# A gated attention and GLU kernel, forward and backward: 34 far attention tiles turned by DMA, filler work spread over the query tiles, K and V in rings of two

## The chip, the cores and the metric

The kernel runs on one core of a Trainium2 chip. The metric is the device time of one execution in microseconds (us); lower is better. The core's engines are TensorE (PE in the profile; its weight loads are PEld), VectorE (DVE), ScalarE (ACT), GpSimd (POOL) and SyncE (SP). SP computes nothing: it issues most of the DMAs, one after the other in the order in which they were written.

## The reference

The program computes a layer's output and the gradients of seven of its inputs. Batch 1, S = 2048 tokens, D = 512, H = 32 heads of 16, attention window W = 256, F = 1376; all in bfloat16.

```python
def A(x, wqkv, wo):                       # sliding-window attention
    q, k, v = (x @ wqkv) split into 32 heads of 16
    scores = q k^T * 16 ** -0.5, kept where 0 <= i - j < 256, else -1e9
    return (softmax(scores) v) @ wo
def B(x, W_gate, W_up, W_down):           # gated MLP
    gate, up = x @ W_gate, x @ W_up
    return (gate * (gate > 0) * up) @ W_down
g = sigmoid((x * gate_w).sum(-1))
out = g * A(x) + (1 - g) * B(x)
# returned: out, and the gradients for grad_out of x, wqkv, wo, W_gate, W_up, W_down, gate_w
```

## The kernel before, in words

There are three stages, one after the other. Their PE work is laid end to end by hand-written lists (`manual_schedule`): every engine executes its instructions in the order in which Python emits them.

**Stage 1 (0 to about 250 us), the MLP.** 44 steps of 128 features by 512 tokens: gate, up, the gradient of h, and the weight gradients. Its last steps also make the first projections for the attention.

**Stage 2 (about 250 to 715 us), the attention forward and backward.** The heads are worked through in four groups c = 0 to 3 of 8 heads, in each 16 query tiles j of 128 tokens. A query tile meets up to three key tiles kb: its own (role d, kb = j), the one before (role m, j - 1) and the far one (role f, j - 2; masked from the other side). Each pair is done in two halves of four heads. One half of one pair is a *unit*; there are 360, six for a full query tile.

A unit runs through these steps, one new unit per round n of the loop:

- round n: `front` (L681) multiplies K by Q into PSUM (ST, PE), ACT takes the exponential into the tile Pu, POOL masks it for the roles d and f;
- round n + 1: `front_dp` (L704) multiplies V by the output's gradient (dPT, PE);
- round n + 2: `gradp` (L712), DVE multiplies Pu by dPT into Pd;
- round n + 4: `rowsum` (L717), row sums, outputs and query gradients (BA), eight small matmuls;
- Pu and Pd have to be turned (keys on the rows, queries on the columns exchanged) for the key and value gradients. `flip` (L735) does it. The two halves of a d pair and of an m pair lie side by side and are turned by one DMA transpose from SP (L743, 128x2048, in round n + 3 of the second half). Far units, and four m units at the end of the last group, are turned by PE: eight 128x128 transposes into PSUM (L753) and one eviction by ACT or DVE (L754, L755), in round n + 4.
- `cd_piece` (L532) multiplies the turned tiles by the small tensor rq into CD, the sums for the key and value gradients of one key tile. A key tile needs its three query tiles; the six pieces are put in a queue `cdq` with the round from which they may run, and one or two are taken per round.

Between the units the loop places *filler work* for PE. `project_parts` (L123) makes the six parts of the next projection: Q, dO, a DMA transpose of rows, K, V, and the transposes for KV1. They belong to a *block* of four query tiles (512 tokens of one head group; 16 blocks in all), and one block ahead is projected. `grad_parts` (L627) makes the gradient of wqkv and wo for the head group before: four sums of four pieces, each piece four matmuls (L641), and a store after each sum.

What is placed when is decided by a `credit`: each round adds 1.5 us, less what the unit itself costs (0.63, and 0.44 where PE turns a tile), and each filler takes its own cost from it. A projection part is taken when the credit is over 0.4 and one round was left free, or when its due round comes; a gradient piece when at most two projection parts are left (L960). `plan` (L620) says after which block's projection which weights of stage 3 are turned or loaded into the slots x0..x3, d0..d3, p0..p3, which the inputs of projections no longer needed leave free; `late` holds them, and they are issued in some rounds only (L966). The rest, `W_rest`, follows after the attention.

The projected K0, K1, V0, V1 and KV1 lie in rings: every third block's in the pool pjA (one buffer), the others' in the pool `pj` (two buffers), so three blocks are alive at a time (L126, L518). The far units have rings Pu and Pd of two buffers each, and their turned tiles P2f a ring of four.

**Stage 3 (about 715 us to the end)** multiplies h by Wdown and o by its gradient, then, per token tile, computes the output and the gradient of x.

Of the kernel before, what the change touches and what calls it, by code (L numbers as in the profile page):

```python
# [11 lines left out]
BF = mybir.dt.bfloat16  # L12
# [10 lines left out]
def kernel(  # L23
# [20 lines left out]
    nc = tc.nc  # L44
    P = 128
# [9 lines left out]
    NT = S // P  # L55
# [56 lines left out]
    if True:  # L112
# [10 lines left out]
        def project_parts(c, tg):  # L123
            t4 = {}
            proj[(c, tg)] = t4
            pj = lambda: pjA if (c * NTG + tg) % 3 == 0 else pjs["b"]  # L126

# [386 lines left out]
    if True:  # L514
        st = p3.enter_context(tc.tile_pool(name="attst", bufs=2))
        gwp = p3.enter_context(tc.tile_pool(name="gwp", bufs=2))
        p3b = ExitStack()
        pjs["b"] = p3b.enter_context(tc.tile_pool(name="pj", bufs=2))  # L518
        wk = p3b.enter_context(tc.tile_pool(name="attw", bufs=2))
# [63 lines left out]
        def clear(name):  # L583
            nc.gpsimd.memset(W6[(name, FC - 1)][0:FC * P - F, :], 0.0)
# [32 lines left out]
        def load_gw():  # L617
# [4 lines left out]
                12: turns("Wg", B_W_gate, 0, 4, "x0") + turns("Wg", B_W_gate, 4, 8, "d0"),  # L622
                15: loads("Wd", B_W_down, 0, "x3") + loads("Wd", B_W_down, 4, "d3") + loads("Wd", B_W_down, 8, "p3")}
        W_rest = (turns("Wg", B_W_gate, 8, 12, "x1") + [lambda: clear("Wg")] + turns("Wu", B_W_up, 0, 4, "d1") + turns("Wu", B_W_up, 4, 8, "x2")
                  + turns("Wu", B_W_up, 8, 12, "d2") + [lambda: clear("Wu")])

# [35 lines left out]
        for c in range(DC):  # L662
            for j in range(NT):
                kbs = [k for k in (j - 1, j, j - 2) if k >= 0]
                for half in range(2):
                    order = kbs if half or len(kbs) < 3 else [kbs[0], kbs[2], kbs[1]]
                    for ki, kb in enumerate(order):
                        u = Unit()
                        u.c, u.j, u.kb, u.half = c, j, kb, half
                        u.first = ki == 0 and half == 0  # L670
                        u.last = ki == len(kbs) - 1 and half == 1
                        u.role = ("d", "m", "f")[j - kb]
                        u.pair = u.role == "d" or (u.role == "m" and (c < DC - 1 or j < NT - 2))
                        u.own = u.role == "f"
                        u.dma = u.pair
                        units.append(u)
# [4 lines left out]
        def front(u):  # L681
# [6 lines left out]
            if not u.own:  # L688
                if u.half == 0:
                    tag = f"PP{u.role}"  # L690
                    pairs[(u.c, u.j, u.kb)] = wk.tile([P, 2, 2, HH, P], BF, tag=tag, bufs=3, name=tag)
                u.PP = pairs[(u.c, u.j, u.kb)][:, u.half, :, :, :]
                u.Pu, u.Pd = u.PP[:, 0, :, :], u.PP[:, 1, :, :]
            else:
                u.Pu = wk.tile([P, HH, P], BF, tag="Pu", bufs=2, name="Pu")
            nc.scalar.activation(u.Pu[:], ST[:], ACT.Exp)  # L696
# [15 lines left out]
        def gradp(u):  # L712
            if u.own:
                u.Pd = wk.tile([P, HH, P], BF, tag="Pd", bufs=2, name="Pd")
            nc.vector.tensor_tensor(out=u.Pd[:], in0=u.Pu[:], in1=u.dPT[:], op=ALU.mult)  # L715
# [19 lines left out]
        def flip(u):  # L735
            key = (u.c, u.j, u.kb, "p2")
            if u.role != "f" and key not in P2 and not (u.pair and u.half == 0):
                P2[key] = wk.tile([P, 2, 2, HH, P], BF, tag=f"P2{u.role}", bufs=3, name=f"p2{u.role}")
            if u.dma:
                if u.pair and u.half == 0:  # L740
                    return
                hs = slice(0, 2) if u.pair else slice(u.half, u.half + 1)
                nc.sync.dma_start_transpose(out=P2[key][:, hs, :, :, :].rearrange("p b a h q -> p (b a h) q"),  # L743
                                            in_=pairs[(u.c, u.j, u.kb)][:, hs, :, :, :].rearrange("p b a h q -> p (b a h q)"))
                for b in range(2)[hs]:
                    P2[(u.c, u.j, u.kb, b)] = P2[key][:, b, :, :, :]
                return
# [3 lines left out]
            for a, src in enumerate((u.Pu, u.Pd)):  # L751
                for hh in range(HH):
                    nc.tensor.transpose(pt[:, a, hh, :], src[:, hh, :], ident[:])  # L753
            p2 = P2[key][:, u.half, :, :, :] if u.role == "m" else wk.tile([P, 2, HH, P], BF, tag="P2f", bufs=4, name="p2")[:]  # L754
            evac(p2, pt[:], eng)  # L755
# [83 lines left out]
        with tc.manual_schedule():  # L839
# [36 lines left out]
            while n <= NU + LAG or ev or cdq or bgq:  # L876
                now = ev.pop(n, [])
                u = units[n] if n < NU else None
                if u is not None:
# [3 lines left out]
                    if u.first and u.j % TPG == 0:  # L883
                        if gi + 1 < len(groups):
                            prq = project_parts(*groups[gi + 1]) if gi else second
                            due = n + sum(2 * min(3, j + 1) for j in range(u.j, u.j + TPG)) - 3
                            if gi + 2 == len(groups):
                                due -= 10
                    if u.first and u.j == TPG and ends:
                        copies.append(ends.pop(0))  # L890
                    if u.first and u.j == 1 and u.c > 0:
                        ready = grad_parts(u.c - 1)
                    if u.first and u.j == TPG - 1 and u.c > 0:
                        bgq += ready
                    front(u)
# [51 lines left out]
                elif held and credit > 0.3:  # L947
                    held = background()
                    credit -= 0.65
                elif prq and not held and ((credit > 0.4 and n > fed + 1) or due - n <= len(prq)):  # L950
                    fed = n
# [6 lines left out]
                    if not prq:  # L958
                        late += plan.get(gi + 1, [])
                elif bgq and len(prq) <= 2 and credit > 0.3:  # L960
                    held = background()
                    credit -= 0.65
# [178 lines left out]
```

## Time and profile before

Three runs took 907.59, 908.57 and 911.35 us, the median is 908.57.

| What | Value |
|---|---|
| Profiled execution, its own time | 907.26 us |
| Its span, first to last instruction | 905.5 us |
| Granted TensorE clock | 1.00 throughout |
| PE busy | 889.5 us, 98% |
| DVE, ACT, POOL busy | 511.1, 445.5, 492.8 us |
| First and last score matmul (ST) of the attention | 249.6 and 697.5 us |
| Head groups 0 to 3, from first ST to the next group's first ST | 101.9, 115.5, 115.9, 114.6 us |
| DMA transposes of d pairs and of m pairs from SP | 64 and 58 |
| Their median time from issue to landing | 5.5 and 5.3 us |
| Transposes by PE of far units (L753) | 896, 112 units of 8 |

A row of the profile that names a line and an engine is a group of equal instructions: what it writes and reads, how many, the busy time, the mean duration in ns, and the idle time of the engine before them with what ended it. SPq is the DMA queue of SP; the duration of its rows is the time for which an issue holds the queue, not the time to the landing. The DMA share of a stretch adds up the times of all packets over 16 DMA engines and can be above 1, since packets overlap.

### The profile page before, as it was taken

How to read it: one execution, taken by the hardware profiler on the slowest of the kernel's cores; microseconds unless marked ns; L12 is line 12 of the kernel's file. 1: busy time of each engine (PE TensorE's matmuls, PEld its weight loads, DVE VectorE, ACT ScalarE, POOL GpSimd, SP SyncE). 2: the span in 40 equal slices, each digit the busy share in tenths (PEclk: the TensorE clock that was granted, in tenths of full speed). 3: DMA queues.
4: the chain of work that ended last, by engine and by line, in shares of the span. 5: the costliest groups of instructions: out<-in, count | busy, mean ns of one | idle time of the engine just before them, and what ended most of it. 6: DMA issues, size and time to landing. Idle time of an engine off the chain costs nothing.

```text
span 905.5 us, 25962 instructions
## 1 busy us (share of the span) xinstructions
PE 889.5 (98%) x10607; PEld 560.2 (62%) x10607; DVE 511.1 (56%) x946; ACT 445.5 (49%) x787; POOL 492.8 (54%) x937
## 2 busy tenths in 40 slices
PE   9999999999989999999999999999999999999998
PEld 5565655655657777677776677766677544444445
DVE  4433334434368887678886788877786101333343
ACT  6422232222278778667776677766787112111111
POOL 4544545545267778767777567876787100222232
PEclk9999999999999999999999999999999999999999
DMA  9998989999799999999999989999999899998940
GB/s 301 204 193 185 198 181 210 215 216 216 180 138 159 190 185 197 185 171 156 175 187 183 184 161 183 187 193 183 192 219 190 222 243 228 275 255 218 189 134 30
DMA packets 520984, 174.57 MB, mean 193 GB/s; under 512 B 446817, under 2 KB 519745, under 8 KB 520865
## 3 DMA queue, kind: packets, MB, share of 16 engines
q1 hardware_dynamic: 498624, 150.62, 89.6%
q10 hardware_dynamic: 20608, 17.70, 7.5%
q0 software_dynamic: 1632, 4.59, 1.5%
q8 instruction: 83, 1.36, 0.6%
q14 instruction: 37, 0.30, 0.1%
HBM read 34.37 MB, written 36.24 MB: 78 GB/s over the span
## 4 chain that ended last, share of the span: by engine, by line
PE 85%; DMA 4%; DVE 4%; ACT 2%; POOL 2%; SPq 2%; issue 1%; ACTq 0%; POOLq 0%; DVEq 0%
PE dxps L1068 8%; PE wps L412 8%; PE ST L687 7%; PE dPT L710 7%; PE pt L753 5%; PE dxps L1072 4%; PE dps L414 4%; PE pp L133 4%; PE dhps L363 4%; PE ups L363 4%; PE CD L541 4%; PE gps L363 4%; PE BA L724 4%; PE wps L641 4%; PE bps L1023 3%; PE BA L726 2%
## 5 line engine op out<-in xcount | busy, mean ns | idle before, releaser
L687 PE MATMUL ST<-z,K 128*128 128x512 bf16 x360 | 135.9, 378 | 3.3 <-ACT PPd L696 1.2
L710 PE MATMUL dPT<-z,V 128*128 128x512 bf16 x360 | 136.0, 378 | 1.8 <-DVE Pd L715 0.5
L698 POOL TENSOR_SCALAR_AFFINE_SELECT PPd<-PPd 128x512 bf16<-128x512 bf16 x128 | 81.3, 636 | 80.1 <-ACT PPd L696 80.0
L377 POOL TENSOR_TENSOR hT<-rg,upm 128x512 bf16<-128x512 bf16 x44 | 51.0, 1160 | 113.8 <-DVE upm L375 97.5
L412 PE MATMUL wps<-dgu_r,x_r 128*128 128x256 bf16 (+1 forms) x704 | 103.9, 270 | 0.0
L715 DVE TENSOR_TENSOR PPd<-PPd,dPT 128x512 bf16<-128x512 bf16 x128 | 86.9, 680 | 19.9 <-PE dPT L710 12.3
L701 POOL TENSOR_SCALAR_AFFINE_SELECT Pu<-Pu 128x512 bf16<-128x512 bf16 x112 | 72.0, 643 | 35.1 <-ACT Pu L696 34.0
L696 ACT ACTIVATE PPd<-ST 128x512 bf16<-128x512 f32 x128 | 77.0, 603 | 23.6 <-PE ST L687 18.8
L715 DVE TENSOR_TENSOR Pd<-Pu,dPT 128x512 bf16<-128x512 bf16 x112 | 76.4, 682 | 21.0 <-PE dPT L710 10.6
L412 PEld LDWEIGHTS <-x_r 128*128 128x128 bf16 x704 | 68.4, 98 | 30.9 <-issue 0.2
L696 ACT ACTIVATE Pu<-ST 128x512 bf16<-128x512 f32 x112 | 67.4, 602 | 37.2 <-PE ST L687 37.1
L715 DVE TENSOR_TENSOR PPm<-PPm,dPT 128x512 bf16<-128x512 bf16 x120 | 80.1, 667 | 7.1 <-PE dPT L710 6.1
L696 ACT ACTIVATE PPm<-ST 128x512 bf16<-128x512 f32 x120 | 72.5, 604 | 16.7 <-PE ST L687 16.2
L375 DVE SCALAR_TENSOR_TENSOR upm<-rg,ups 128x512 bf16<-128x512 bf16 x44 | 30.2, 685 | 81.8 <-ACT rg L369 43.1
L369 ACT ACTIVATE rg<-gps 128x512 bf16<-128x512 f32 x44 | 26.3, 597 | 89.0 <-PE gps L363 47.4
L414 PE MATMUL dps<-db_r,h_r 128*128 128x512 bf16 x176 | 66.8, 379 | 0.0
L1048 ACT COPY a_sb<-aps 128x512 f32<-128x512 f32 x16 | 9.4, 585 | 108.0 <-issue 99.8
L72 ACT COPY p<-pt 128x1024 bf16<-128x1024 bf16 x59 | 60.1, 1019 | 4.2
L387 POOL TENSOR_TENSOR dgu<-dh_sb,rg 128x512 bf16<-128x512 bf16 x44 | 58.0, 1318 | 5.3 <-ACT dh_sb L383 5.3
L386 DVE TENSOR_TENSOR dgu<-dh_sb,upm 128x512 bf16<-128x512 bf16 x44 | 34.5, 784 | 29.8 <-ACT dh_sb L383 26.1
L641 PE MATMUL wps<-rows_st,x_r 128*128 128x384 bf16 x256 | 50.3, 325 | 0.0
L133 PE MATMUL pp<-x,p 128*128 128x512 bf16 x192 | 49.0, 378 | 0.0
(178 smaller groups left out, 2323.2 us busy)
## 6 DMA issues: line engine op xcount, KB each, us to landing
dqkvo_d<-rows_st SPq DMA_DIRECT2D x15, 512.0 KB, 4.3
hT_d<-hT ACTq DMA_DIRECT2D x44, 128.0 KB, 2.5
dgT_d<-dgu ACTq DMA_DIRECT2D x44, 128.0 KB, 2.9
duT_d<-dgu ACTq DMA_DIRECT2D x44, 128.0 KB, 3.0
h<-hT_d SPq DMA_DIRECT2D x8, 640.0 KB, 4.9
dgT_g<-dgT_d SPq DMA_DIRECT2D x8, 640.0 KB, 5.2
duT_g<-duT_d SPq DMA_DIRECT2D x8, 640.0 KB, 6.5
go_g<-in_grad_out_dram SPq DMA_DIRECT2D x16, 256.0 KB, 4.7
```

The source lines that it names most:

```text
L133: nc.tensor.matmul(pp[:], lhsT=w_p[c][:, cd, which * P:(which + 1) * P], rhs=x_T[tg][:, cd, :], start=(cd == 0), stop=(cd == DC - 1))
L363: nc.tensor.matmul(out[:], lhsT=w(c), rhs=x(c), start=(c == 0), stop=(c == DC - 1))
L412: nc.tensor.matmul(acc["w"][:, c, 0:2 * nw], lhsT=x_r[:, t, c * P:(c + 1) * P], rhs=k.dgu_r[:, :, i, s0:P], start=(go_ and c % 2 == 0), st ...
L414: nc.tensor.matmul(acc["d"][:], lhsT=k.h_r[:, i, :], rhs=db_r[:, t, :], start=go_, stop=no_)
L641: nc.tensor.matmul(wps[:], lhsT=x_r[:, t, part * P:(part + 1) * P], rhs=sts[c][:, t, 0:3, :], start=first and t == t0, stop=last and t == ...
L687: nc.tensor.matmul(ST[:], lhsT=KTt[:, ksl], rhs=z[:, 0, :, jl, :], start=True, stop=True)
L696: nc.scalar.activation(u.Pu[:], ST[:], ACT.Exp)
L698: nc.gpsimd.affine_select(out=u.Pu[:], in_=u.Pu[:], compare_op=ALU.is_ge, fill=0.0, base=0, pattern=[[0, HH], [1, P]], channel_multiplier=-1)
L701: nc.gpsimd.affine_select(out=u.Pu[:], in_=u.Pu[:], compare_op=ALU.is_ge, fill=0.0, base=-1, pattern=[[0, HH], [-1, P]], channel_multiplier=1)
L710: nc.tensor.matmul(u.dPT[:], lhsT=VTt[:, ksl], rhs=z[:, 1, :, jl, :], start=True, stop=True)
L715: nc.vector.tensor_tensor(out=u.Pd[:], in0=u.Pu[:], in1=u.dPT[:], op=ALU.mult)
L1068: nc.tensor.matmul(to, lhsT=src[:, fc, lsl], rhs=W6[(wt, fc)][:, cols], start=(fc == 0 and wt == "Wg"), stop=False)
```

## The change

- 34 of the 112 far units are turned by DMA: in group 0 the first half (`half == 0`) of query tiles 4, 6, 8, 10, 12, 14, in groups 1 and 2 that of tiles 3, 4, 5, 6, 8, 9, 10, 12, 13, 14, in group 3 that of tiles 3, 4, 5, 6, 8, 9, 10, 12. Each gets a DMA transpose of its own from SP, 128x1024, in round n + 3 instead of n + 4. The other 78 are still turned by PE.
- Pu and Pd of a far unit lie side by side in one tile PF with a ring of four; the ring P2f has five buffers.
- K, V and KV1 have rings of two: even blocks in pjA, odd blocks in `pj` with one buffer. The last three parts of a projection (K, V, KV1's transposes) wait for round `gate`, 12 rounds into the block (5 in a head group's first block).
- The 16 gradient pieces of the head group before are put in the queue four at a time, at the query tiles 3, 5, 9 and 13, instead of all at tile 3. They may also run while three projection parts wait for the gate. The last projection's due round is 6 earlier than the rule instead of 10.
- The rows of Wdown are loaded after the projections of blocks 13 and 14 into the slots x1, d1 and x2 instead of after block 15 into x3, d3 and p3; the weights of `W_rest` get the slots d2, x3, d3, p3.

```diff
-            pj = lambda: pjA if (c * NTG + tg) % 3 == 0 else pjs["b"]
+            pj = lambda: pjA if (c * NTG + tg) % 2 == 0 else pjs["b"]
...
-        pjs["b"] = p3b.enter_context(tc.tile_pool(name="pj", bufs=2))
+        pjs["b"] = p3b.enter_context(tc.tile_pool(name="pj", bufs=1))
...
-                15: loads("Wd", B_W_down, 0, "x3") + loads("Wd", B_W_down, 4, "d3") + loads("Wd", B_W_down, 8, "p3")}
-        W_rest = (turns("Wg", B_W_gate, 8, 12, "x1") + [lambda: clear("Wg")] + turns("Wu", B_W_up, 0, 4, "d1") + turns("Wu", B_W_up, 4, 8, "x2")
-                  + turns("Wu", B_W_up, 8, 12, "d2") + [lambda: clear("Wu")])
+                13: loads("Wd", B_W_down, 0, "x1") + loads("Wd", B_W_down, 4, "d1"), 14: loads("Wd", B_W_down, 8, "x2")}
+        W_rest = (turns("Wg", B_W_gate, 8, 12, "d2") + [lambda: clear("Wg")] + turns("Wu", B_W_up, 0, 4, "x3") + turns("Wu", B_W_up, 4, 8, "d3")
+                  + turns("Wu", B_W_up, 8, 12, "p3") + [lambda: clear("Wu")])
...
-                        u.dma = u.pair
+                        u.dma = u.pair or (u.own and half == 0 and j in ((4, 6, 8, 10, 12, 14), (3, 4, 5, 6, 8, 9, 10, 12, 13, 14), (3, 4, 5, 6, 8, 9, 10, 12, 13, 14), (3, 4, 5, 6, 8, 9, 10, 12))[c])
...
-                u.Pu = wk.tile([P, HH, P], BF, tag="Pu", bufs=2, name="Pu")
+                u.PP = wk.tile([P, 2, HH, P], BF, tag="PF", bufs=4, name="PF")
+                u.Pu, u.Pd = u.PP[:, 0, :, :], u.PP[:, 1, :, :]
...
         def gradp(u):
-            if u.own:
-                u.Pd = wk.tile([P, HH, P], BF, tag="Pd", bufs=2, name="Pd")
             nc.vector.tensor_tensor(out=u.Pd[:], in0=u.Pu[:], in1=u.dPT[:], op=ALU.mult)
...
+            if u.dma and u.own:
+                p2 = wk.tile([P, 2, HH, P], BF, tag="P2f", bufs=5, name="p2f")
+                nc.sync.dma_start_transpose(out=p2[:].rearrange("p a h q -> p (a h) q"),
+                                            in_=u.PP[:].rearrange("p a h q -> p (a h q)"))
+                P2[(u.c, u.j, u.kb, u.half)] = p2[:]
+                return
             if u.dma:
...
-            p2 = P2[key][:, u.half, :, :, :] if u.role == "m" else wk.tile([P, 2, HH, P], BF, tag="P2f", bufs=4, name="p2")[:]
+            p2 = P2[key][:, u.half, :, :, :] if u.role == "m" else wk.tile([P, 2, HH, P], BF, tag="P2f", bufs=5, name="p2")[:]
...
                             if gi + 2 == len(groups):
-                                due -= 10
+                                due -= 6
+                            gate = n + (12 if u.j else 5)
...
-                    if u.first and u.j == TPG - 1 and u.c > 0:
-                        bgq += ready
+                    if u.first and u.c > 0 and u.j in (3, 5, 9, 13):
+                        bgq += ready[:NT // 4]
+                        del ready[:NT // 4]
...
-                elif prq and not held and ((credit > 0.4 and n > fed + 1) or due - n <= len(prq)):
+                elif prq and not held and (len(prq) > 3 or n >= gate) and ((credit > 0.4 and n > fed + 1) or due - n <= len(prq)):
...
-                elif bgq and len(prq) <= 2 and credit > 0.3:
+                elif bgq and (len(prq) <= 2 or len(prq) == 3 and n < gate) and credit > 0.3:
```

## The prediction

> **What bounds the kernel now.** I read the page first: whether one engine is full throughout, and the chain of waits.
>
> ```profile
> span 905.5 us, 25962 instructions
> PE 889.5 (98%) x10607; PEld 560.2 (62%) x10607; DVE 511.1 (56%) x946; ACT 445.5 (49%) x787; POOL 492.8 (54%) x937
> ...
> PE 85%; DMA 4%; DVE 4%; ACT 2%; POOL 2%; SPq 2%; issue 1%; ACTq 0%; POOLq 0%; DVEq 0%
> ```
>
> PE (TensorE) is busy 98% of the span and makes 85% of the chain. Busy overlaps in pipelined matmuls, so I priced PE by the distance from one start to the next in the timeline. Then the stage table: the four query tiles 8 to 11 of head group 1, one row each (a row's third number is PE's busy time, the last but one the DMA share).
>
> ```profile
> 411.20:418.80 7.60, 7.60 (x138) 5.23 (x135) 5.53 (x10) 5.23 (x10) 5.27 (x13) 1.00 1.03 150
> 418.80:427.10 8.30, 8.26 (x145) 5.72 (x143) 8.16 (x18) 6.10 (x12) 5.83 (x15) 1.00 0.96 170
> 427.10:433.20 6.10, 6.10 (x133) 4.64 (x130) 5.36 (x11) 5.21 (x10) 5.30 (x13) 1.00 1.23 167
> 433.20:439.10 5.90, 5.90 (x131) 4.47 (x128) 4.70 (x8) 5.05 (x10) 5.26 (x13) 1.00 1.31 187
> ```
>
> The first two tiles carry the next block's projection (three parts each), the last two none; PE is full in all four, and the transfers are crowded where filler is missing. The DMA queue itself (SP) in that stretch:
>
> ```profile
> 428.17 2.64 SPq L743 DMA_TRANSPOSE p2m<-PPm  x1
> 430.91 3.22 SPq L743 DMA_TRANSPOSE p2d<-PPd  x1
> 434.23 2.45 SPq L743 DMA_TRANSPOSE p2m<-PPm  x1
> 436.79 3.20 SPq L743 DMA_TRANSPOSE p2d<-PPd  x1
> ```
>
> One transpose follows the next within 0.1 to 0.2 us: 5.7 us of queue in a 5.9 us tile. SP is the second bound. That it already reaches PE once, near the end of the attention, two rows of the waits show:
>
> ```profile
> ACT PPd L696 <- DMA p2d<-PPd: 2.2, 1, 2.2
> ...
> PE CD L541 <- DMA p2m<-PPm: 0.5, 1, 0.5
> ```
>
> **The change, part by part.** What a far unit costs on PE today, in the timeline, and its eviction and transposes in the groups by shape:
>
> ```profile
> 400.11 0.38 PE L753 MATMUL pt<-ident,Pu 128*128 128x128 bf16 x4
> 400.33 0.39 PE L753 MATMUL pt<-ident,Pd 128*128 128x128 bf16 x4
> 400.55 0.38 PE L710 MATMUL dPT<-z,V 128*128 128x512 bf16 x1
> ...
> L72 ACT COPY p<-pt 128x1024 bf16<-128x1024 bf16 x59 | 60.1, 1019 | 4.2
> L74 DVE COPY p<-pt 128x1024 bf16<-128x1024 bf16 x53 | 36.3, 686 | 11.3 <-PE pt L753 10.9
> ```
>
> Removed: eight transposes from 400.11 to the next matmul at 400.55, 0.44 us of PE, in 34 units: 15.0 us, all on PE and so on the path. 34 evictions of 1.02 (ACT) or 0.69 us (DVE) go too; neither engine is the bound (DVE's worst row above is 8.16 of 8.30, where a projection's spreads, K and V meet; the new order puts K and V two tiles after the spreads), so I count them zero; were DVE the bound there, 0.69 a unit would be a gain.
>
> Added: 34 DMA transposes of 128x1024 on SP. The rows of the queue (min/median/max ns):
>
> ```profile
> L743 SPq DMA_TRANSPOSE p2d<-PPd x64: 1774/2566/3814, 253.2 to 702.4; - x64
> L743 SPq DMA_TRANSPOSE p2m<-PPm x58: 1650/2886/4358, 257.8 to 690.9; - x58
> ...
> L181 SPq DMA_TRANSPOSE rows<-zT x16: 1232/1280/1962, 232.1 to 653.9; - x16
> ```
>
> `rows` has the far unit's very size: 1.28 us. Half of a pair's 2.72 (64 x 2.57 + 58 x 2.89 = 332 us over 122) gives 1.36. I take 1.3, as the nearest row is the same shape: 34 x 1.3 = 44 us of queue. Does it fit? I added up SP's rows from the first score matmul of each head group to that of the next: 84.3 us of 101.9, 96.0 of 115.5, 98.6 of 115.9 and 109.1 of 114.6. PE alone would shorten the groups by 0.44 us for each of their 6, 10, 10 and 8 far units: 99.3, 111.1, 111.5, 111.1. The queue needs 92.1, 109.0, 111.6 and 119.5. So group 0 fits, groups 1 and 2 fit to the brim (98 and 100%), group 3 is 8.4 us over.
>
> What is queued behind a far transpose: the middle and own pairs of the same tile, the stores, the spill, the weight turns. Who waits: CD matmuls read a far tile ten units after its issue (about 12 us), a pair's tile 12 to 15 units after. The landing takes 3.3 us (`rows`), so a lag of some 6 us costs nothing; beyond that CD, or the exponential that reuses the buffer, stands. I let half of group 3's excess (4.2 us) go into that lag, because it must drain before the attention ends. Bounds: 0 (all of it is lag) and 8.4.
>
> At full queue the fit can't be perfect: in group 3, tiles 2 to 5, SP is 35.3 of 36.8 us busy and PE loses 2.3 us against its own sum. At that rate, half of it for groups 1 and 2 (223 us), which are as full but steadier: 223 x 2.3/36.8 / 2 = 7; bounds 0 and 14. I take 3.4, since the tiles without filler above run at 96% of SP without loss.
>
> Moved, with one answer: the gradient pieces (16 per group, four matmuls from start to start 0.16 us each, 0.65 us a piece) and K, V and their transposes. Their count stays; PE's sum by block of four tiles goes, following the credit rule through the loop, from 33.8, 27.3, 27.3 us to 28.6 in each of tiles 4-7, 8-11, 12-15 (tiles of 7.1, 8.0, 7.6 and 5.9 us). In groups 1 to 3 far transposes go with filler tiles; group 3's tile 12 has none. It costs PE nothing while SP keeps up; without that cover, each far transpose beside an unfilled 5.9 us tile would cost about 1.1 us. Stores of the four sums move with their last pieces (SP 0.6 to 1 us each, counted above).
>
> K and V in rings of two: K, V and the memset of KV1 now wait for the last readers of the block before last. The gate puts them 12 units into the block (score matmuls of the old tile end at 11, BA at 15, the memset comes at 16), so nobody should stand; POOL queues selects and the small products behind the memset. Cost 0; bound 14 blocks x 0.3 us (one KV memset's row) = 4 us if it is always late, below nothing not, since it adds only waits.
>
> Wdown rows into x1, d1, x2: the same bytes, issued in tiles 4 to 8 of group 3 instead of 10 to 11. It takes about 2.4 us of stall away at 683 to 690 (the two waits above) and lays the transfers on the fullest block. I put it at 0, bounds -2.4 and +4.8 (three issues at 1.6 us, the longest that such a load held SP).
>
> The new buffers (PF four deep, P2f five) give a far unit 12 units before reuse: 0.
>
> **Sum**: -15.0 + 4.2 + 3.4 = -7.4 us. The profiled execution took 907.26 (span 905.5 and 1.8 around it): 899.9. The median is 908.57, 1.3 above: **901**. A measurement of this kernel tells about 0.5%, 4.5 us.
>
> Here a page speaks for more. The Trainium skill, Advanced Engine Details and Errata, section X-Bar Transpose (TRN2), expects 350 to 400 GB/s of transposes; by that a far unit would be an estimated 0.7 us of queue and all 15 us would stay. A pair's 512 KB in 2.72 us is 193 GB/s; the trace does not agree.
>
> **The rivals.**
> - *PE keeps all* (queue lag is always absorbed): -15 to -17 us with the late stall, 892. For it: tiles at DMA share 1.31 ran without a PE wait. Against: group 3's 119.5.
> - *The queue eats the gain*: the waits of CD take over what PE saved, within 4.5 us of 908.6. For it: SP full in three of four groups.
> - *The queue becomes the bound* (slower): all SP rows but pairs are 388 - 332 = 56 us, so attention needs 139 pair-equivalents (122 + 34/2) at a us each, plus 56. It decides at a = 2.82, where that is 448 us, the attention's time now. The mean is 2.72, which gives 434; but where SP runs solid, from 669 to 697, eight pairs hold 25.3 us, 3.17 each. At a = 2.92, 462: +14, 922. Against: the dense tiles above hold a pair in 2.88 with PE undisturbed, and removing PE instructions removes fetches that interrupt transfers.
> - *The rings bind*: K waits on readers, +4 on the forecast, 905.
>
> The Trainium skill, Perfetto Trace Analysis, section What "DMA-bound" means, calls a kernel bound by the DMA sequencer when its track is solid DMA slices. By that rule the dense tiles are bound already, and the third rival would hold; the row of 5.90 us PE busy in 5.90 says not yet.
>
> **How the numbers follow.** Forecast (896 to 904) 0.36; PE keeps all 0.16; eaten 0.20; queue bound 0.25; rings 0.03. Faster by over 0.5%: 0.36 + 0.16 = 0.52. Same: 0.20 + 0.03 = 0.23. Slower: 0.25. The range runs from 890 (PE keeps all, -17 and a little) to 919 (a = 2.90): outside lie about 0.05 below and 0.12 above. The likeliest case's own range is 896 to 904.
>
> **What will show it.** Right: 624 instead of 896 far transposes on PE (112 - 34 = 78 units); 34 new SP transposes of about 1.3 us; tiles 8 to 11 of a group near 28.6 us, with PE full; group 3 longer than its PE sum, with CD waiting for p2f, p2m or p2d, or ACT for p2d. Wrong: pairs on SP over 2.8 us in the mean, waits of CD or of the exponentials on DMA in groups 1 and 2, or K, V, KV1 waiting on PE.

## The result, and the profile after

The change makes the kernel slower. Five runs after it took 933.63 to 940.77 us, median 936.31; five runs of the kernel before, on the same chip, 907.14 to 911.35, median 908.01. The ratio is 1.0312, with a 95% interval of [1.0291, 1.0333]. The forecast was 901.0 with a range of 890 to 919, so sign and range were both wrong. The profiled execution of the changed kernel took 940.77 us, 4.5 above its median; its span is 938.8.

First the page of the changed kernel: the span, the engines, the start of the chain, and the granted clock in 40 slices.

```profile
span 938.8 us, 25373 instructions
PE 884.5 (94%) x10233; PEld 552.3 (59%) x10335; DVE 492.4 (52%) x930; ACT 426.9 (45%) x769; POOL 490.0 (52%) x937
...
PEclk9999999999999999999999999899898999999999
...
PE 23%; DMA 3%; SPq 1%; ACT 0%; issue 0%; DVE 0%; POOL 0%; ACTq 0%
```

PE is busy for 884.5 us instead of 889.5, and for 94% of the span instead of 98%: it now waits. That its busy time fell by 5.0 us and not by the 15.0 saved has two reasons: part of its work ran at a lower clock (last section), and some matmul records are missing from the trace (10233 against 10335 weight loads). The recorded chain is cut short (27% of the span), so I read no shares from it. New is the clock: it is below 0.9 in three slices, late in the attention.

Now the four query tiles 8 to 11 of head group 1, which were the stage table of the prediction (start and length, the busy times of PE, PEld, DVE, ACT and POOL with counts, granted clock, DMA share, GB/s).

```profile
411.40:419.40 8.00, 7.32 (x127) 4.91 (x126) 5.33 (x10) 4.88 (x9) 5.05 (x12) 1.00 1.09 187
419.40:427.60 8.20, 8.16 (x133) 5.62 (x133) 6.70 (x13) 5.19 (x10) 5.16 (x12) 1.00 1.18 218
427.60:435.40 7.80, 7.69 (x136) 5.37 (x135) 5.13 (x12) 5.36 (x11) 6.08 (x15) 1.00 1.12 163
435.40:443.50 8.10, 6.27 (x127) 4.59 (x125) 5.37 (x12) 4.91 (x10) 4.96 (x12) 1.00 1.15 181
```

They take 32.1 us, against 27.9 before and 28.6 in the forecast, and in the first and the last of them PE is not full (7.32 of 8.00, 6.27 of 8.10). The four head groups, in the same columns:

```profile
251.70:354.10 102.40, 97.09 (x1702) 67.24 (x1714) 78.06 (x153) 78.33 (x141) 76.90 (x180) 1.00 1.09 177
354.10:474.30 120.20, 111.91 (x1916) 77.23 (x1928) 84.39 (x163) 78.15 (x145) 83.86 (x197) 0.99 1.15 189
474.30:596.20 121.90, 113.40 (x1916) 77.89 (x1927) 84.55 (x163) 77.18 (x144) 83.90 (x197) 0.97 1.17 191
596.20:730.90 134.70, 115.14 (x1914) 79.35 (x1920) 81.46 (x154) 77.72 (x142) 83.74 (x195) 0.91 1.13 195
```

The time came from here: 102.4, 120.2, 121.9 and 134.7 us instead of 101.9, 115.5, 115.9 and 114.6, in sum 31 us more, and most of it in group 3 (the two profiled executions are 33.5 us apart, the medians 28.3). What PE and the engine before it waited for:

```profile
ACT PF L697 <- DMA p2f<-PF: 22.0, 8, 6.4
...
PE dPT L711 <- ACT PF L697: 19.5, 9, 6.0
PEld L541 <- DMA p2f<-PF: 18.7, 6, 6.1
ACT PPd L697 <- DMA p2d<-PPd: 15.2, 6, 4.6
...
PE dPT L711 <- ACT PPd L697: 10.2, 4, 3.5
```

Each row gives the total wait in us, how many times, and the longest. The exponential (ACT, L697) waits for a transpose to have read the buffer that it wants to fill, or CD's weight load for the turned tile; then PE stands for up to 6 us. Before, the two such rows came to 2.2 and 0.5 us. One of the longest, first on ACT, then on PE, then on SP over the same stretch:

```profile
650.96 0.60 ACT L697 ACTIVATE PPm<-ST 128x512 bf16<-128x512 f32 x1 [0.29 <-PE BA L725]
657.96 0.60 ACT L697 ACTIVATE PF<-ST 128x512 bf16<-128x512 f32 x1 [6.40 <-DMA p2f<-PF]
```

```profile
652.42 0.17 PE L725 MATMUL BA<-KV,PPd 128*128 128x17 bf16 x1
658.61 0.58 PE L711 MATMUL dPT<-z,V 128*128 128x512 bf16 x1 [6.02 <-ACT PF L697]
```

```profile
645.68 3.21 SPq L748 DMA_TRANSPOSE p2m<-PPm  x1
648.99 1.96 SPq L748 DMA_TRANSPOSE p2d<-PPd  x1
651.00 1.75 SPq L581 DMA_TRANSPOSE d<-in_B_W_gate_dram  x1
652.85 1.50 SPq L740 DMA_TRANSPOSE p2f<-PF  x1
654.45 3.89 SPq L748 DMA_TRANSPOSE p2m<-PPm  x1
658.45 1.94 SPq L748 DMA_TRANSPOSE p2d<-PPd  x1
660.44 0.99 SPq L606 DMA_DIRECT2D x<-in_B_W_down_dram  x1
661.53 1.25 SPq L740 DMA_TRANSPOSE p2f<-PF  x1
```

SP has no gap longer than 0.11 us. The far transpose issued at 652.85 landed 5.0 us later, at 657.9, and the exponential started at 657.96. The queue is late by more than the rings hold, and PE follows the queue. By the Trainium skill, Perfetto Trace Analysis, section What "DMA-bound" means, a kernel is bound by the DMA sequencer when its track is solid DMA slices; this stretch agrees, with a solid SP and PE standing for 6.02 us. It does not tell whether the queue itself or the transfer engines behind it keep the rows long. The solid tiles of the kernel before, with PE full in them, were the edge of that state.

The rows of the transposes themselves (min/median/max ns in the queue):

```profile
L740 SPq DMA_TRANSPOSE p2f<-PF x34: 1246/1636/2694, 276.3 to 713.2; - x34
...
L748 SPq DMA_TRANSPOSE p2m<-PPm x58: 1785/3016/4968, 259.0 to 721.8; - x58
...
L748 SPq DMA_TRANSPOSE p2d<-PPd x64: 1712/2524/4043, 255.3 to 733.3; - x64
```

A far unit holds the queue for 1.64 us in the median and 1.71 in the mean, where I had 1.3. The pairs are 2.74 us in the mean, hardly changed from 2.72.

### The profile page after: what moved, and what is told of

Read it like the earlier page. It is cut to its first block, busy times and chain, and to the rows that moved or that the text cites. A ratio compares the mean times of both kernels' runs of the same rounds, so it can differ in the third digit from the quotient of the medians.

```text
span 938.8 us, 25373 instructions
## 1 busy us (share of the span) xinstructions
PE 884.5 (94%) x10233; PEld 552.3 (59%) x10335; DVE 492.4 (52%) x930; ACT 426.9 (45%) x769; POOL 490.0 (52%) x937
## 5 line engine op out<-in xcount | busy, mean ns | idle before, releaser
L711 PE MATMUL dPT<-z,V 128*128 128x512 bf16 x360 | 140.0, 389 | 31.3 <-ACT PF L697 19.5
L687 PE MATMUL ST<-z,K 128*128 128x512 bf16 x360 | 139.6, 388 | 5.2 <-ACT PF L697 1.7
L412 PE MATMUL wps<-dgu_r,x_r 128*128 128x256 bf16 (+1 forms) x704 | 103.9, 270 | 1.6 <-DVE wst L74 0.8
L697 ACT ACTIVATE PF<-ST 128x512 bf16<-128x512 f32 x112 | 67.9, 606 | 59.9 <-PE ST L687 32.7
L697 ACT ACTIVATE PPd<-ST 128x512 bf16<-128x512 f32 x128 | 77.4, 606 | 36.8 <-PE ST L687 20.3
L702 POOL TENSOR_SCALAR_AFFINE_SELECT PF<-PF 128x512 bf16<-128x512 bf16 x112 | 72.4, 646 | 41.0 <-ACT PF L697 40.0
L714 DVE TENSOR_TENSOR PF<-PF,dPT 128x512 bf16<-128x512 bf16 x112 | 76.5, 683 | 31.2 <-POOL PF L702 24.0
L697 ACT ACTIVATE PPm<-ST 128x512 bf16<-128x512 f32 x120 | 72.1, 601 | 25.5 <-PE ST L687 23.5
L414 PE MATMUL dps<-db_r,h_r 128*128 128x512 bf16 x159 | 60.3, 379 | 0.0
L758 PE MATMUL pt<-ident,PF 128*128 128x128 bf16 x624 | 49.0, 223 | 0.0
L541 PEld LDWEIGHTS <-p2d 128*128 128x128 bf16 x512 | 36.9, 97 | 19.2 <-issue 14.1
L133 PE MATMUL pp<-x,p 128*128 128x512 bf16 x153 | 45.7, 388 | 2.1 <-issue 0.5
```

The source lines that it names most:

```text
L412: nc.tensor.matmul(acc["w"][:, c, 0:2 * nw], lhsT=x_r[:, t, c * P:(c + 1) * P], rhs=k.dgu_r[:, :, i, s0:P], start=(go_ and c % 2 == 0), st ...
L414: nc.tensor.matmul(acc["d"][:], lhsT=k.h_r[:, i, :], rhs=db_r[:, t, :], start=go_, stop=no_)
L687: nc.tensor.matmul(ST[:], lhsT=KTt[:, ksl], rhs=z[:, 0, :, jl, :], start=True, stop=True)
L702: nc.gpsimd.affine_select(out=u.Pu[:], in_=u.Pu[:], compare_op=ALU.is_ge, fill=0.0, base=-1, pattern=[[0, HH], [-1, P]], channel_multiplier=1)
L711: nc.tensor.matmul(u.dPT[:], lhsT=VTt[:, ksl], rhs=z[:, 1, :, jl, :], start=True, stop=True)
```

## The experiments

The theory after the result: SP's queue is the bound of the attention. It needs more time than the attention lasted before, so PE's saving is worth nothing, and each added transpose lengthens the attention. Rivals: the other three edits cost the time (order, rings, Wdown); or the turned far tiles come too late for their readers, which would be a matter of dependence and not of load.

### The other edits alone

```diff
-                        u.dma = u.pair or (u.own and half == 0 and j in ((4, 6, 8, 10, 12, 14), (3, 4, 5, 6, 8, 9, 10, 12, 13, 14), (3, 4, 5, 6, 8, 9, 10, 12, 13, 14), (3, 4, 5, 6, 8, 9, 10, 12))[c])
+                        u.dma = u.pair
```

> The changed kernel with all 112 far units turned by PE again; the three other edits stay (gradient sums in four parts, rings of two with the gate, Wdown slots). Queue theory (the 34 far transposes overfill the DMA queue, the rest is harmless): PE's work is that of the kernel before and the queue is as free as there, 902 to 910 us, no waits for p2f, waits of the exponentials on p2d under 3 us. Rival (the rings and the gate, or the moved filler, cost the time): at least half of the 28 us stays, 920 us or more, with K, V or KV waiting on PE.

Measured: 911.17 us, ratio 1.0023 [1.0008, 1.0038]. Order, rings and Wdown together cost 0.2%; the 34 far units cost the rest, nearly 3%. The rivals on the other edits fall.

### The load without the benefit

34 transposes of the same size that nobody reads, issued for the same 34 units (`extra` marks them), on top of the kernel just shown; the ring PF has two buffers instead of four, to make room. PE still turns every far unit.

```diff
+                if 3 <= n < NU + 3 and units[n - 3].extra:
+                    xt = wk.tile([P, 2 * HH, P], BF, tag="XT", bufs=2, name="xt")
+                    nc.sync.dma_start_transpose(out=xt[:], in_=x_r[:, 0:2, :].rearrange("p a d -> p (a d)"))
```

> All far units are turned by PE, and in the 34 places SP issues a transpose of the same size from a constant tile (x_r) into a scratch tile that nobody reads; the ring PF has two buffers instead of four to make room. Queue theory (it is the queue's time that is missing, whoever needs the result): SP again 95% busy in groups 1 to 3 and 930 to 950 us, as slow as the changed kernel or slower, since PE saves nothing. Rival (what hurts is that the far tile itself comes late to CD and that its buffer is held): the queue takes 44 to 58 us more without harm, 902 to 915 us.

Measured: 936.17 us, ratio 1.0298 [1.026, 1.0337], the changed kernel's time (1.0312 [1.0291, 1.0333]). It makes no difference whether anybody waits for the far tile, nor whether PE is spared 34 x 8 transposes. The waits show the same queue, now at the pairs alone:

```profile
ACT PPd L698 <- DMA p2d<-PPd: 18.8, 10, 4.7
...
PEld L541 <- DMA p2m<-PPm: 13.9, 9, 3.0
...
PE CD L541 <- DMA p2m<-PPm: 11.2, 8, 2.7
```

So the load explains the loss, and not the lateness of the far tiles as such.

### All 112 far units by DMA

```diff
-                        u.dma = u.pair or (u.own and half == 0 and j in ((4, 6, 8, 10, 12, 14), (3, 4, 5, 6, 8, 9, 10, 12, 13, 14), (3, 4, 5, 6, 8, 9, 10, 12, 13, 14), (3, 4, 5, 6, 8, 9, 10, 12))[c])
+                        u.dma = u.pair or u.own
```

> All 112 far units are turned by DMA, 78 more than in the changed kernel. Queue theory: each costs the queue about 1.71 us, and with the queue full at 95.5% each adds 1.75 to 1.8 us to the attention: 936 + 78 x 1.78 = 1075 us (1050 to 1100), PE busy under 85%. Rival (lag of single tiles, and PE saves 0.44 us in each): under 1000 us.

Measured: 1037.82 us (one run), between the two forecasts (1050 to 1100, and under 1000). 78 more units cost 101.5 us, 1.30 each, although each spares PE 0.44. The queue theory asked too much because the rows are shorter here: a far unit holds the queue 1.57 us in the mean instead of 1.71, a pair 2.59 instead of 2.74. The head groups take 129.9, 144.1, 146.0 and 159.5 us, and PE waits for the queue:

```profile
PEld L541 <- DMA p2f<-PF: 125.8, 44, 6.8
PE CD L541 <- DMA p2f<-PF: 118.7, 42, 6.7
```

### Fewer far units

12 units (group 0 at tiles 6, 10, 14, the others at 5, 9, 13), and 26 (none in group 3):

```diff
-  ((4, 6, 8, 10, 12, 14), (3, 4, 5, 6, 8, 9, 10, 12, 13, 14), (3, 4, 5, 6, 8, 9, 10, 12, 13, 14), (3, 4, 5, 6, 8, 9, 10, 12))[c]
+  ((6, 10, 14), (5, 9, 13), (5, 9, 13), (5, 9, 13))[c]
```

```diff
-  (3, 4, 5, 6, 8, 9, 10, 12, 13, 14), (3, 4, 5, 6, 8, 9, 10, 12))[c]
+  (3, 4, 5, 6, 8, 9, 10, 12, 13, 14), ())[c]
```

> Only 12 far units by DMA: in group 0 tiles 6, 10, 14, in groups 1 to 3 tiles 5, 9, 13, the fullest tile of each block (PE 7.6 and 8.0 us). Queue theory: SP needs about 101 us of 114 in groups 1 and 2, which fits, group 3 is full as before; PE saves 12 x 0.44 = 5.3 us less a part in group 3: 2 to 5 us under the kernel with none, 898 to 907 us. Rival (a far tile turned by DMA comes late wherever it stands): at or above the kernel with none, waits of CD on p2f of 0.5 us each, +6 us or more.

> The changed kernel without the 8 far transposes of head group 3; the 26 of groups 0 to 2 stay. Queue theory: groups 0 to 2 as in the changed kernel (102, 120, 122 us), group 3 back to 114 to 119 us, since it inherits a lag and is 95% full by itself: 917 to 923 us. Rival (the loss of group 3 is the sum of lag that groups 1 and 2 leave): group 3 stays over 125 us, 927 us or more.

Measured: 915.24 us, ratio 1.006 [1.0038, 1.0082], and 924.64 us, ratio 1.0171 [1.0151, 1.019]. Both lie above what the queue theory gave (898 to 907, and 917 to 923), and below what its rivals gave (6 us or more above the kernel with none, and 927 or more). With 12 units, groups 0 to 2 take 103.9, 114.7 and 114.3 us, against 103.9, 115.6 and 116.0 without far units: 2.6 us less for 9 units (PE's 0.44 would give 4.0). Group 3 takes 121.3 instead of 114.2, 2.4 us for each of its three units; part of that may be lag from group 2, for the next run shows a group 3 that loses time without a unit of its own. In the changed kernel the 8 units of group 3 cost 936.31 - 924.64 = 11.7 us, 1.5 each; without them the group takes 120.4 us (114 to 119 was expected). Group 3 had no room at all: without far units its queue rows already come to 109.3 of 114.2 us.

### Where SP idles, in the kernel before

The kernel before with nothing but 10 far units by DMA, in tiles where SP idled, and none in group 3; the rings PF and P2f get three buffers.

```diff
-                        u.dma = u.pair
+                        u.dma = u.pair or (u.own and half == 0 and j in ((5, 9, 13), (5, 7, 9, 13), (7, 9, 13), ())[c])
...
-                u.Pu = wk.tile([P, HH, P], BF, tag="Pu", bufs=2, name="Pu")
+                u.PP = wk.tile([P, 2, HH, P], BF, tag="PF", bufs=3, name="PF")
```

> The kernel before with 10 far units by DMA, each in a query tile in whose time SP was idle for 1.8 to 3.6 us (group 0: 5, 9, 13; group 1: 5, 7, 9, 13; group 2: 7, 9, 13; none in group 3); rings PF and P2f of three in the old space; filler order, K and V rings and Wdown slots as before. Queue theory: 10 x 1.5 to 1.7 us fit into the idle queue time of these tiles, PE saves 10 x 0.44 = 4.4 us: 903 to 907 us, 0.2 to 0.6% under the kernel before. Rival (P2f of three buffers holds the evictions up, or a far tile is late wherever it stands): 908 to 915 us.

Measured: 911.52 us, ratio 1.0028 [1.0016, 1.004]. The queue theory's 903 to 907 missed: the units do not fit into the idle time. The time lies in its rival's 908 to 915, but not for the ring of three that the rival named: the evictions wait for PE's transposes alone. In group 0 a tile with a far unit becomes 0.3 to 0.5 us shorter (tile 9: 7.89 us instead of 8.19; tile 13: 7.85 instead of 8.33), as PE's saving says, and the dense tiles behind it lose more (tiles 10 and 11: 6.31 and 6.77 instead of 6.10 and 5.97; tiles 14 and 15: 6.35 and 6.42 instead of 5.90 and 5.97). The transposes do not stay in the tile where SP idles: they delay the pairs that come after them. Group 3, which has none, takes 117.8 us instead of 114.6.

### Six units in the roomiest group

```diff
-  ((4, 6, 8, 10, 12, 14), (3, 4, 5, 6, 8, 9, 10, 12, 13, 14), (3, 4, 5, 6, 8, 9, 10, 12, 13, 14), (3, 4, 5, 6, 8, 9, 10, 12))[c]
+  ((4, 6, 8, 10, 12, 14), (), (), ())[c]
```

> The changed kernel with only group 0's six far units by DMA; the 28 of groups 1 to 3 are turned by PE. SP has room in group 0 only (82.0 of 103.9 us in the kernel without far units by DMA, 911.2 us). Theory A, a far unit saves PE 0.44 us where the queue has room: 6 x 0.44 = 2.6 us in group 0, and the time is 908.5 to 910, with groups 1 to 3 as without far units (115.6, 116.0, 114.2). Theory B, the saving never arrives, or the group's lag runs on into group 1: 911 or more. The difference is near what can be told apart; the groups' lengths in the trace decide with it.

Measured: 913.09 us, ratio 1.0042 [1.0027, 1.0058]. By the times it can't be told from the kernel without far units (1.0023 [1.0008, 1.0038]), but the gain of theory A (908.5 to 910) is excluded: the lower end of the interval, 1.0027 times the 909.35 us of the kernel before beside it, is 911.8. The trace shows why. Group 0 does become shorter, 102.5 instead of 103.9 us. Group 1, which has no far unit by DMA, becomes longer: 119.8 instead of 115.6. Its query tile 1 takes 8.57 us instead of 5.16, and tile 2 9.10 instead of 8.24. SP in this kernel, over the border at 353.7:

```profile
346.83 2.05 SPq L748 DMA_TRANSPOSE p2m<-PPm  x1
348.99 2.23 SPq L748 DMA_TRANSPOSE p2d<-PPd  x1
351.31 2.72 SPq L740 DMA_TRANSPOSE p2f<-PF  x1
354.14 2.01 SPq L748 DMA_TRANSPOSE p2m<-PPm  x1
356.25 2.56 SPq L748 DMA_TRANSPOSE p2d<-PPd  x1
358.98 3.60 SPq L748 DMA_TRANSPOSE p2m<-PPm  x1
```

ACT in the same stretch:

```profile
361.94 0.60 ACT L697 ACTIVATE PPd<-ST 128x512 bf16<-128x512 f32 x1 [3.97 <-DMA p2d<-PPd]
```

From group 0's tile 7 to its end SP is 59.4 of 62.4 us busy. The last far transpose, 2.72 us at 351.31, is issued late, so the first pairs of group 1 are late too, and group 1's tiles 0 and 1 have little PE work and much to turn (in the kernel without far units SP is 4.82 of 5.16 us busy in tile 1). There the lag of the queue becomes a wait. The same tile 1 of groups 1, 2 and 3 takes 8.71, 8.95 and 9.43 us in the changed kernel, against 5.16, 5.08 and 5.08: 11.8 us, over a third of the loss, at three places.

### What of a transpose costs: its size, its number, or the turning

On the kernel with 34 unread transposes: 17 of twice the size (same bytes, half the issues, at every other place), 34 of half the size, and 34 plain copies of the same 256 KB.

```diff
-                    nc.sync.dma_start_transpose(out=xt[:], in_=x_r[:, 0:2, :].rearrange("p a d -> p (a d)"))
+                    nc.sync.dma_start_transpose(out=xt[:], in_=x_r[:, 0:4, :].rearrange("p a d -> p (a d)"))
```

```diff
-                    nc.sync.dma_start_transpose(out=xt[:], in_=x_r[:, 0:2, :].rearrange("p a d -> p (a d)"))
+                    nc.sync.dma_start_transpose(out=xt[:], in_=x_r[:, 0, :])
```

```diff
-                    nc.sync.dma_start_transpose(out=xt[:], in_=x_r[:, 0:2, :].rearrange("p a d -> p (a d)"))
+                    nc.sync.dma_start(xt[:].rearrange("p a q -> p (a q)"), x_r[:, 0:2, :].rearrange("p a d -> p (a d)"))
```

> As the run with 34 unread transposes of 128x1024, but with 17 of 128x2048: the same bytes, half as many issues. If the bytes fill the queue (the DMA engines' time): again 930 to 940 us. If each issue has a cost of its own (a far transpose holds the queue 1.71 us, half a pair 1.37): 17 issues of 2.74 instead of 34 of 1.69, 11 us less queue, 922 to 928 us.

> The kernel without far units by DMA (911.2 us), plus 34 unread transposes of half the size, 128x512, in the same places (at 128x1024 they gave 936.2). The computation is whole; the transposes are extra. Theory A, queue time binds and up to some 15 us of it are free, since SP idled 47 us in the kernel without them and 18 in the one with 12 far units: 34 times about 0.85 us are 29 us of queue, and the time is 914 to 922, less than half of the 25 us. Theory B, the number of transposes is what costs (each issue disturbs): near 936, at least 930. A straight line in bytes without any free part would give 923.7.

> The kernel without far units by DMA (911.2 us), plus 34 unread plain copies of 256 KB, SBUF to SBUF, issued by SP in the places where the unread transposes stood (those gave 936.2, a far-sized transpose holding the queue 1.69 us). The computation is whole; the copies are extra. Theory A, the turning itself is what is slow: a plain copy of the same bytes holds the queue well under 1.69 us, say 0.7 to 1.0, so the attention needs 23 to 34 us less of queue, and the time is 911 to 920. Theory B, any 256 KB that passes through the DMA engines costs the same: 1.5 us or more each and 930 to 940.

Measured: 936.17 us (ratio 1.0297 [1.0275, 1.032]), 929.98 (1.0204 [1.0169, 1.0238]) and 922.66 (1.0129 [1.0098, 1.016]). The copies' row in the queue:

```profile
L921 SPq DMA_DIRECT2D xt<-x_r x34: 508/586/1464, 275.4 to 697.7; - x34
```

Halving the number at the same bytes saves nothing, as the theory of bytes said (930 to 940). Halving the bytes at the same number saves a quarter to a third of the loss: 18.8 of 25.0 us are left by the times, 1.8 of 2.75% by the ratios (beside these runs the kernel before took 909.93 us, beside the kernel without far units 908.95). So the first theory on that run (914 to 922) fell and the second (at least 930) was just missed; the median rows go with the second: 1.45 us for 128x512, 1.67 for 128x1024, 3.20 for 128x2048. Below 128x1024 a transpose holds the queue almost as long.

A plain copy holds it for 0.59 us, about a third, yet costs 11.5 us (1.1% by the ratios), two fifths to a half of the loss: a little above what the first theory on it gave, and far below the second. In that kernel the other rows grow: the mean pair goes from 2.73 to 2.87 us in group 1 and from 2.68 to 2.85 in group 2. Against the same pairs in the kernel without far units, the 19 pairs issued directly behind a copy hold the queue 0.46 us longer in the mean (0.11 behind an unread transpose), the 85 with no copy beside them 0.02. So a copy's own row is not its price. By time the turning is the larger part of what a transpose costs. By queue rows it is the smaller: against the kernel without far units the 34 copies add 44.5 us and the 34 transposes of the same bytes 62.6. Part of the copies' 44.5 us fell into time in which SP would have idled; its gaps of 0.35 us and more shrink from 48 to 12 us in all.

The Trainium skill, Advanced Engine Details and Errata, section X-Bar Transpose (TRN2), calls transposes as fast as regular DMAs; in this queue the trace does not agree, with 1.67 against 0.59 us for 256 KB, and medians of 4.6 against 3.5 us from issue to landing.

### Wdown's rows in their old and their new slots

The changed kernel with the Wdown edit taken back, and the kernel before with only that edit (the inverse diff):

```diff
-                13: loads("Wd", B_W_down, 0, "x1") + loads("Wd", B_W_down, 4, "d1"), 14: loads("Wd", B_W_down, 8, "x2")}
+                15: loads("Wd", B_W_down, 0, "x3") + loads("Wd", B_W_down, 4, "d3") + loads("Wd", B_W_down, 8, "p3")}
```

> The changed kernel with the Wdown rows loaded where the kernel before loads them (after block 15, slots x3, d3, p3, and the slots of the other weights with them). Queue theory: the same bytes pass through the same full queue in group 3, only some tiles later: within 5 us of the changed kernel, 931 to 941 us, group 3 again 130 to 138 us, the long stall moved from tile 7 to tiles 10 to 12. Rival (group 3's 20 us come from the loads' new place): 920 to 928 us.

> The kernel before with only the other slots and issue places of Wdown's rows. The computation is whole. In the changed kernel taking this edit back gave 4.7 us (936.3 to 931.6). Theory A, the three loads cost because the queue is full where they are issued; in the kernel before, SP has idle time there except in the fullest tiles of the last group, so it is 906 to 910, within 0.3%. Theory B, the new places cost by themselves (the weights of the last stage come later, or their slots free later): 911 to 914.

Measured: 931.57 us (ratio 1.0247 [1.0228, 1.0266]) and 909.76 (0.9998 [0.9982, 1.0015]). With the queue overfull the edit costs 4.7 us (0.65%, or 5.9 us, by the ratios); in the kernel before it costs nothing. In these two kernels the place of the loads has no price of its own, only one beside a late queue. The stall did not move as expected: with the old slots the long tiles of group 3 are 6 and 7 (13.0 and 11.3 us), not 10 to 12, and the group takes 128.5 us, less than the 130 to 138 expected.

### All kernels side by side

Queue rows are the sum of SP's rows from the first to the last ST, the attention is that stretch; both are worked out from the traces. The times were taken on several chips, on which the kernel before took 908.0 to 909.9 us.

| Kernel | Queue rows, us | Attention, us | Share | Time, us |
|---|---|---|---|---|
| other edits alone | 386.4 | 449.7 | 86% | 911.17 |
| before | 388.0 | 447.9 | 87% | 908.01 |
| 6 units in group 0 | 402.3 | 453.4 | 89% | 913.09 |
| before + 10 units | 411.9 | 453.1 | 91% | 911.52 |
| 12 units | 417.0 | 454.2 | 92% | 915.24 |
| 34 plain copies | 430.9 | 461.0 | 93% | 922.66 |
| 26 units | 436.2 | 463.9 | 94% | 924.64 |
| 34 half transposes | 441.9 | 468.6 | 94% | 929.98 |
| after, old Wdown slots | 442.3 | 470.0 | 94% | 931.57 |
| 34 unread transposes | 449.0 | 475.9 | 94% | 936.17 |
| after | 450.9 | 479.1 | 94% | 936.31 |
| 17 double transposes | 452.5 | 477.9 | 95% | 936.17 |
| all 112 units | 547.2 | 579.6 | 94% | 1037.82 |

From 436 us of rows on, the attention is the queue rows divided by 0.94 to 0.95, whatever the transfers are for. Most of the missing 5 to 6% is not idle time that more work could fill: in the changed kernel 209 gaps of less than 0.35 us between consecutive rows, 0.09 us each in the mean, hold 19.6 us, and all longer gaps together 8.6; with all 112 units the short gaps are again 0.09 us each. Between 388 and 430 us the curve bends: the attention grows though SP still idles in places.

No kernel beat the one before.

Two things stay open. No run issued its transposes from a second queue, so it is not shown whether SP's queue or the transfer engines behind it are what is full; the DMA share of the head groups is 1.03 to 1.13 before the change and 1.09 to 1.17 after it. And the granted clock stood at half for 34.1 us of the changed kernel's attention, but for 17.1 us with 34 unread transposes, which take as long. So the loss does not follow the clock; how much of it a full clock would give back was not tried.

## Why the prediction was wrong

- **What was right.** The instruction counts (624 far transposes left on PE, 34 new ones on SP); K, V and KV1 in rings of two, at nothing (the other edits alone cost 0.2%); the place of the trouble, group 3; and who would wait (CD for the far tile, the exponential for the pairs). SP was named as the second bound, and the list of signs named waits in groups 1 and 2 as the mark of an error; they came. Pairs over 2.8 us, the other mark, did not come (2.74).
- **The far unit at 1.3 us.** The term that was mis-sized first. I took the median row of 16 transposes of the same shape (1.28; their mean in the trace is 1.39) and half a pair (1.36). In the full queue the mean is 1.71: 34 x 0.41 = 14 us of queue more. The range in the rows I had shown (up to 1.96 for `rows`, up to 4.36 for a pair) allowed for it. The pair's 2.72 was added up from two medians, and by luck is the true mean. That fewer PE instructions would help the transfers, as the case against the third rival had it, does not show: the instruction queue moved 81 packets instead of 83, and a pair takes 2.74 us instead of 2.72.
- **"Groups 1 and 2 fit to the brim (98 and 100%)", and 3.4 us for the imperfect fit.** The largest error, and the step that failed. I let the queue fill to 100% and took 3.4 us for the rest. The table shows that it fills to 94 or 95%. The loss of 2.3 us from which I scaled that term is not in the trace: in tiles 2 to 5 of group 3 PE idles 1.3 us (35.49 of 36.80 busy), and in the same tiles of group 2 0.8 us, so it held no measure of a full queue. For the attention I forecast 432.0 us of queue rows (388.0 + 44) in 440.5 us; it had 450.9 in 479.1. Of the 38.6 us between, 18.9 are more rows (14 of them the far units above) and 19.7 are more queue time without a row (28.2 instead of 8.5). The third rival's own sum was nearly right: 139 pair-equivalents at (122 x 2.74 + 34 x 1.71) / 139 = 2.82 us, and 56, make 448 us of queue. It called that the point from which it decides; at 0.94 the point lies at 421 us of rows, or 2.63 a pair, and the forecast's own 432 was already beyond it. With the measured 2.82 and the 0.94, the rival's sum gives 477 us of attention; it was 479.1.
- **The sum by head groups.** "Group 0 fits" (92.1 of 99.3) averaged a light beginning with a full end. The run with six units in group 0 shows 95% over its last nine tiles, 1.4 us gained in the group and 4.2 lost in the next one. Queue time that is idle early in a group is of no use to transposes that come late in it.
- **"A lag of some 6 us costs nothing"**, and half of group 3's excess absorbed (4.2). The lag does not drain while the queue stays full; it is handed to the next tiles, at the latest to tiles 0 and 1 of the next group, which are the densest (tile 1 has two pairs, 5.5 us at the mean, in 5.1 to 5.2 us). I had looked at who reads a tile, and said that beyond the lag CD or the exponential stands, but I had not asked where the queue has time to catch up.
- **-15.0 us of PE.** The saving is real where the queue is not late (0.3 to 0.5 us in the tiles with a far unit) and worth nothing elsewhere: with the load alone and no saving the time was the same.
- **The new buffers at 0.** With a late queue the largest wait stands at that very ring: the exponential waits 22.0 us, in 8 times, for a far transpose to have read its tile PF. It is where the lateness shows and no price of its own, for with unread transposes, where that wait is absent, the time is the same.
- **Wdown at 0, bounds -2.4 and +4.8.** It cost 4.7 us in the full queue (5.9 by the ratios), at the upper bound or over it, and 0 in the kernel before.

In shares of the time before, from the ratios: the other edits 0.2%, group 0's six units 0.2%, the 20 of groups 1 and 2 1.3%, the 8 of group 3 1.4%, together 3.1%.

## What to carry to other kernels

When work moves from a full engine to a second resource that is 87% busy, price it by the second resource: its need divided by the share at which it really runs full (here 0.94), compared tile by tile and not by the mean over a stage. Idle time in a serial queue is usable only if the queue catches up before the next dense stretch; look for the stretch with the least cover behind the added work, for the delay arrives there. Two cheap runs tell load from benefit: the added transfers with nobody reading them, and the same kernel without them.

## What the runs showed of the hardware that was not expected

**The granted clock falls after PE has stood.** In the kernel before it was 1.00 in every head group; in the changed one 0.99, 0.97 and 0.91 in groups 1 to 3, and 0.85 to 0.91 in all four with 112 units. After the stand of 6.02 us shown above, PE in the changed kernel:

```profile
660.91 0.63 PE L711 MATMUL dPT<-z,V 128*128 128x512 bf16 x1
661.34 0.64 PE L687 MATMUL ST<-z,K 128*128 128x512 bf16 x1
661.76 0.64 PE L711 MATMUL dPT<-z,V 128*128 128x512 bf16 x1
...
663.71 0.38 PE L711 MATMUL dPT<-z,V 128*128 128x512 bf16 x1
663.93 0.18 PE L541 MATMUL CD<-rq,p2d 128*128 128x32 bf16 x1
```

From start to start a 128x512 matmul takes 0.43 us here and 0.22 again from 663.71 on. So a stand costs its own length and some of the work after it. A shorter one does too: with six units in group 0, tiles 1 and 2 of group 1 (same columns as the tables above), where PE stood for 2.85 us,

```profile
356.30:364.80 8.50, 5.65 (x104) 3.69 (x101) 5.27 (x12) 3.98 (x9) 3.43 (x8) 0.92 1.10 187
364.80:373.90 9.10, 8.84 (x139) 5.56 (x135) 6.02 (x15) 5.90 (x13) 7.62 (x20) 0.88 1.12 208
```

and the same tiles without far units by DMA:

```profile
356.30:361.40 5.10, 5.05 (x104) 3.65 (x102) 4.19 (x10) 3.93 (x9) 2.69 (x6) 1.00 1.01 209
361.40:369.70 8.30, 7.97 (x140) 5.37 (x138) 7.32 (x18) 6.01 (x13) 7.91 (x20) 1.00 1.18 206
```

Tile 2 has the same work and no stand, and takes 0.8 us longer at 0.88. The Trainium skill, TensorE: Matmul & The Clock Gate, Part 1, has the clock halved once PE was idle for a window of about 3.4 us, and full again after about as long; the doubled distances agree, and so does the return some 4 to 5 us after PE went on at 658.61. The stand of 2.85 us is shorter than that window, and the clock fell all the same. In narrow stretches of the kernel with six units (PE went on at 362.59), the granted clock (the last column but two) reads:

```profile
360.00:363.50 3.50, 0.91 (x26) 0.79 (x26) 1.53 (x5) 1.56 (x3) 0.63 (x1) 1.00 1.02 223
363.60:366.90 3.30, 3.30 (x39) 1.77 (x38) 2.10 (x5) 2.21 (x5) 1.92 (x5) 0.50 1.00 217
367.00:373.90 6.90, 6.64 (x119) 4.59 (x117) 4.82 (x12) 4.89 (x10) 5.59 (x16) 1.00 1.12 192
```

So it was half for about 3.4 us and full on both sides. The length of the stand alone does not decide it: after 1.73 us (in the kernel with the old Wdown slots) the clock was 0.50 from 439.2 to 442.5 us, after 1.75 us (in the changed kernel, at 437.5) it stayed at 1.00. What else counts, no run here shows.

**A copy slows its neighbours.** 34 copies, 22 us of queue in their own rows, lengthened the attention by 11.3 us, although without them 63 of 449.7 us of it had no row in the queue. Half of what they added to the queue rows (44.5 us) stands in other rows, 8.7 us of it in the 19 pairs directly behind a copy. What in the transfer engines is shared between a copy and a transpose was not tried; it stays open.
